# Attention, soft MoE and a gated product: the first pairs' loads, squares and stackings in another order

## The chip, the cores and the metric

The kernel runs on one core of a Trainium2 chip. The metric is the device time of one execution in microseconds, as the median of several runs. The engines are called by the profile's names: PE multiplies matrices, DVE, ACT and POOL work element by element, and SP issues the transfers.

## The reference, cut to what matters

```python
def _attn_ref(q, k, v, g_q, g_k):            # q, k, v: 4 x 12 x 448 x 64, float32
    def rmsnorm(x, g):
        rms = np.sqrt(np.mean(x * x, axis=-1, keepdims=True) + 1e-06)
        return x / rms * g
    q_n, k_n = (rmsnorm(q, g_q), rmsnorm(k, g_k))
    scores = scale * np.matmul(q_n, k_n.transpose(0, 1, 3, 2))
    scores = scores - np.max(scores, axis=-1, keepdims=True)
    attn = np.exp(scores)
    attn = attn / (np.sum(attn, axis=-1, keepdims=True) + 1e-09)
    return np.matmul(attn, v)
```

The result, as 1792 tokens of 768 values, goes through a soft mixture of 8 experts of 4 slots each (two softmaxes over the same logits, two products for each expert) and then through `(x @ w_a) * (x @ w_b) @ w_out` with an inner size of 1536. The change touches the attention alone.

## The kernel before, in words

**Tiling.** The 48 heads are 24 pairs. For a pair, q and k are loaded as one slot of `qk_sb` (112 partitions, 512 values of q and 512 of k; three slots take turns), v as one tile. Then, for q and for k: the squares (`square`), their sums by head and token (`sumsq`, tile `ssq`), the inverse root (`rsqrt`, tiles `nt` and `rinv`; ACT makes Ln and Exp, DVE refines it in three small steps, lines L288, L290 and L292), the product with it (`normalise`, tile `n`, L301), four transposes on PE and a split into a high and a low part (`emit_T`, tile `e`, lines L325 to L331), and six transfers from `e` into the two stacked tiles `z` of the pair's heads (`emit_Z`, lines L343 to L345), which is called the stacking here. `e` has one buffer, or two with the second pair's.

**The loop.** A head has four blocks of 112 queries, so a pair has eight steps. A step n issues `score(n + 2)` (two products, L358 and L359, and the maximum on DVE, L360), `expo(n + 1)` (the exponential on ACT, L369) and `ptrans(n)` (four transposes, L382, and an eviction by ACT or, in steps 1 and 5, by DVE). Around these the program puts the products with v of the pair before, and the preparation of pairs 2 to 4 ahead. In steps 5 and 7 the sums for pair j + 4 are taken; their squares are made by POOL (L255).

**Before the loop** the preparation of pairs 0 to 3 is written out: loads of pairs 0 to 2, squares by ACT (`prep`), roots (`norm`), `normalise`, `emit_T` and `emit_Z` of pairs 0 and 1, the load of pair 4 ahead of the second pair's stacking in SP's queue, then 15 products whose result nobody reads (`warm`, `W1`), the roots of pairs 2 and 3 and the first two scores.

**Order.** On PE, ACT, POOL and SP the attention's instructions stand in the order in which the program is written. DVE's order is made by a scheduler when the kernel is built. Every engine works through its own row strictly from the front.

Of the kernel before, what the change touches and what calls it, by code (L numbers as in the profile page):

```python
# [10 lines left out]
F32 = mybir.dt.float32  # L11
# [4 lines left out]
ALU = mybir.AluOpType  # L16
# [16 lines left out]
def kernel(  # L33
    ctx: ExitStack,
    tc: tile.TileContext,
    q: bass.AP,
    k: bass.AP,
    v: bass.AP,
    g_q: bass.AP,
    g_k: bass.AP,  # L40
# [5 lines left out]
):  # L46
    nc = tc.nc
    pe, act, dve, pool, sp = nc.tensor, nc.scalar, nc.vector, nc.gpsimd, nc.sync
    B, H, S, D = q.shape
    NT, DM = out.shape  # L50
    E, F = w1.shape[0], 1024
    NS = phi.shape[1]
    DF = 128 * len(LAGS)
    NC = 4
    P = S // NC
    HP = H // 2
    NPAIR = B * HP
    KD = DM // 128
# [21 lines left out]
    W3 = 2  # L80
    W4 = 7
    W5 = 3
    W1 = 15
    DV = 7
    P2_ENGINES = {ET.PE, ET.SP}

# [6 lines left out]
    ident = const.tile([128, 128], F32, name="ident")  # L93
# [10 lines left out]
    gg, g4, l_run, tb, ssq_eps = few[:, 0:1], few[:, 1:3], few[:, 3:4], few[:, 4:6], few[:, 6:7]  # L104
# [78 lines left out]
    def warm(ps, n):  # L183

        for _ in range(n):
            pe.matmul(ps[:, 0:128], ident, ident, start=True, stop=True)

    cring = ctx.enter_context(ExitStack())
    qk_sb = xw[1]
    extra = cring.enter_context(tc.tile_pool(name="extra", bufs=1)).tile([128, 3072], F32, name="extra")  # L190
    with ExitStack() as c1:
# [28 lines left out]
        def load_qk(p):  # L220
            if p >= NPAIR:
                return
            b, hp = divmod(p, HP)
            t = qk_sb[0:P, p % 3 * 1024:(p % 3 + 1) * 1024].rearrange("p (i h x) -> p i h x", i=2, h=2)
            for i, src in enumerate((q, k)):
                sp.dma_start(out=t[:, i], in_=src[b, 2 * hp:2 * hp + 2].rearrange("h (p c) d -> p h (c d)", c=NC))
            qk_t[p] = t

        def load_v(p):
            if p >= NPAIR:  # L230
                return
            b, hp = divmod(p, HP)
            src = v[b, 2 * hp:2 * hp + 2].rearrange("h (p c) d -> p h c d", c=NC)
            if p < NPAIR - 1:
                t = vp.tile([P, 2, NC, D], F32, tag="v", name=f"v{p}")
                sp.dma_start(out=t, in_=src)
                v_t[p] = [t[:, hd] for hd in range(2)]
            else:
                x = tk.tile([128, S], F32, tag="l4", name="v23a", bufs=1)[0:P, 0:NC * D]
                y = tk.tile([P, 4, 2, 32], F32, tag="c2", name="v23b", bufs=1)  # L240
                v_t[p] = x.rearrange("p (c d) -> p c d", d=D), y.rearrange("p c (a e) s -> p c (a e s)", a=2)
                for hd in range(2):
                    sp.dma_start(out=v_t[p][hd], in_=src[:, hd])

        sq_t = {}

        def square(p, i, eng=None):
            if p >= NPAIR:
                return
            sq = sqp.tile([P, 512], F32, tag="sq", name="sq")  # L250
            a = qk_t[p][:, i].rearrange("p h x -> p (h x)")
            if eng is act:
                act.activation(out=sq, in_=a, func=AF.Square)
            else:
                pool.tensor_tensor(out=sq, in0=a, in1=a, op=ALU.mult)  # L255
            sq_t[p, i] = sq
# [38 lines left out]
        def normalise(p, eng=None):  # L295
            if p >= NPAIR:
                return
            assert not any(x[0] == p for x in small)
            n_t[p] = npp.tile([P, 2, NC, 2, D], F32, tag="n", name=f"n{p}")
            for i in range(2):  # L300
                (eng if eng and i == 0 else pool).tensor_tensor(  # L301
                    out=n_t[p][:, i].rearrange("p c h d -> p h c d"),
                    in0=qk_t[p][:, i].rearrange("p h (c d) -> p h c d", d=D),
                    in1=rinv_t[p][:, i, :].rearrange("p (h c) -> p h c", h=2).unsqueeze(3).to_broadcast(
                        [P, 2, NC, D]
                    ),
                    op=ALU.mult,
                )
            qk_t.pop(p)

        def emit_T(p, i):
            if p >= NPAIR:
                return
            if i == 0:
                if p == 1:
                    e_t[p] = ring_p.tile([128, NU], F32, tag="wu", name="e1").bitcast(F32R)[:, 0:4 * S].rearrange(
                        "p (x s) -> p x s", s=S
                    )
                else:
                    e_t[p] = ep.tile([128, 4, S], F32R, tag="e", name=f"e{p}")  # L320
            et = e_t[p]
            src = n_t[p]
            ps = ps_m.tile([128, 512], F32, tag="m", name="pst")[:, 0:S]
            for c in range(NC):
                pe.transpose(ps[:, c * P:(c + 1) * P], src[:, i, c].rearrange("p h d -> p (h d)"), ident[0:P, 0:P])  # L325
            if i == 0:
                act.activation(out=et[:, 0], in_=ps, func=AF.Copy)
                dve.tensor_tensor(out=et[:, 3], in0=ps, in1=et[:, 0].bitcast(F32), op=ALU.subtract)
            else:
                act.activation(out=et[:, 1], in_=ps, func=AF.Copy, scale=gg)  # L330
                dve.scalar_tensor_tensor(  # L331
                    out=et[:, 2], in0=ps, scalar=gg, in1=et[:, 1].bitcast(F32), op0=ALU.mult, op1=ALU.subtract
                )
                n_t.pop(p)

        def emit_Z(p):
            if p >= NPAIR:
                return
            et = e_t.pop(p)
            for hd in range(2):  # L340
                z = zt[(2 * p + hd) % NZ]
                src = et[hd * D:(hd + 1) * D].bitcast(F32)
                sp.dma_start(out=z[0:D, 0:3].bitcast(F32), in_=src[:, 0:3])  # L343
                sp.dma_start(out=z[D:128, 0].bitcast(F32), in_=src[:, 3])
                sp.dma_start(out=z[D:128, 1:3].bitcast(F32), in_=src[:, 1:3])  # L345
# [201 lines left out]
        def norm(p):  # L547
            rsqrt(p)
            tick(3)

        def prep(p):
            for i in range(2):
                square(p, i, act)
                sumsq(p, i)
# [4 lines left out]
        for i, g in enumerate((g_q, g_k)):  # L559
            for r in range(2):  # L560
                sp.dma_start(out=g4[r * D:(r + 1) * D, i:i + 1], in_=g.rearrange("(d o) -> d o", o=1))
        dve.scalar_tensor_tensor(
            out=gg, in0=g4[:, 0:1], scalar=float(D) ** 0.5, in1=g4[:, 1:2], op0=ALU.mult, op1=ALU.mult
        )
        load_qk(2)
        load_v(0)
        sp.dma_start(out=phi_sb, in_=phi.rearrange("(k p) s -> p k s", p=128))
        prep(0)
        norm(0)
        prep(1)  # L570
        normalise(0, dve)
        load_qk(3)
        emit_T(0, 0)
        emit_T(0, 1)
        emit_Z(0)
        norm(1)
        normalise(1, dve)
        load_qk(4)
        prep(2)
        emit_T(1, 0)  # L580
        emit_T(1, 1)
        emit_Z(1)
        warm(ps_s.tile([128, 512], F32, tag="s", name="warm"), W1)
        norm(2)
        normalise(2)
# [595 lines left out]
            split(i + 2)  # L1181


_INS = ["q", "k", "v", "g_q", "g_k", "moe_phi", "moe_w1", "moe_w2", "moe2_w"]
_OUTS = [((1792, 768), "float32")]


# [35 lines left out]
```

## Time and profile before

| what | value |
|---|---|
| median of 3 runs | 591.48 us (590.6 to 592.62) |
| the profiled execution: its own time | 593.33 us |
| its span, first to last instruction | 591.5 us |
| PE busy | 557.4 us, 94% |
| ACT busy, DVE busy, POOL busy | 359.6, 349.6, 114.0 us |

The time of an execution is 1.9 us more than the span of its instructions. A share of busy time is a mean over stages: in the first 25 us PE waits for others, in the rest of the attention it hardly waits, and from about 330 us on the weights' transfers and then PE again set the pace.

### The profile page before, as it was taken

The page shows a single profiled execution, that of the slowest core. Times are in us where ns is not written, and L with a number is a line of the kernel's source. Part 1 is how long each engine was busy: PE and PEld are TensorE (multiplying, and loading weights), DVE is VectorE, ACT ScalarE, POOL GpSimd, SP SyncE. Part 2 cuts the span into 40 slices and gives each one's busy share as a digit, 9 for nine tenths or more (in the row PEclk, how much of TensorE's full clock was granted, in tenths as well). Part 3 has the DMA queues.
Part 4 walks back from the last instruction along what each step waited for, and adds up shares of the span by engine and source line. Part 5 has one row for each costly group of instructions (what it writes and reads, how often), then busy time and mean ns, then how long its engine had stood idle before and what let it go on. Part 6 is the DMA issues. An engine that isn't in the chain of part 4 may idle for free.

```text
span 591.5 us, 10977 instructions
## 1 busy us (share of the span) xinstructions
PE 557.4 (94%) x3980; PEld 366.9 (62%) x3980; DVE 349.6 (59%) x703; ACT 359.6 (61%) x845; POOL 114.0 (19%) x136
## 2 busy tenths in 40 slices
PE   5989999999999999999999998898989999999997
PEld 5755555566565665655656554343665656689996
DVE  5877777678787687776767521122228888842210
ACT  4677787787887787877877721111169899432210
POOL 1233433333433333333110000010100000200000
PEclk9899999999999999999999999989989999999999
DMA  7955677788697978697676689999999993002332
GB/s 176 220 142 140 165 175 168 209 235 223 165 261 153 266 178 240 166 271 188 156 216 170 271 330 351 426 395 425 428 423 421 418 406 144 1 28 80 92 94 83
DMA packets 39573, 134.51 MB, mean 227 GB/s; under 512 B 5856, under 2 KB 25312, under 8 KB 33120
## 3 DMA queue, kind: packets, MB, share of 16 engines
q1 hardware_dynamic: 39520, 133.81, 72.0%
q8 instruction: 32, 0.52, 0.4%
q14 instruction: 21, 0.17, 0.1%
HBM read 95.26 MB, written 5.51 MB: 170 GB/s over the span
## 4 chain that ended last, share of the span: by engine, by line
PE 75%; DMA 10%; DVE 4%; ACT 4%; SPq 3%; issue 2%; ACTq 0%; DVEq 0%
PE psv L396 12%; PE pspt L382 11%; PE pss L358 5%; DMA z<-e 5%; PE pss L359 5%; PE psM L938 5%; DMA wu_w<-in_moe_w_dram 5%; PE pso L1138 3%; PE pso L1140 3%; PE pso L1139 3%; PE psS L721 3%; PE psh L697 3%; PE pst L325 3%; PE psS L938 2%; PE psx L509 2%
## 5 line engine op out<-in xcount | busy, mean ns | idle before, releaser
L360 DVE TENSOR_REDUCE nmx<-pss 112x1 f32<-112x448 f32 x192 | 118.4, 619 | 40.9 <-PE pss L359 40.5
L369 ACT ACTIVATE p<-pss,nmx 112x448 f32<-112x448 f32 x192 | 123.7, 644 | 9.2 <-DVE nmx L360 6.3
L382 PEld LDWEIGHTS pspt<-ident,p 112*112 112x112 f32 x768 | 80.4, 133 | 78.9 <-ACT pt L388 27.5
L382 PE MATMUL pspt<-ident,p 112*112 112x112 f32 x768 | 110.0, 266 | 1.5 <-ACT p L369 1.4
L388 ACT COPY pt<-pspt 112x448 f32<-112x448 f32 x144 | 76.9, 534 | 27.1 <-PE pspt L382 25.6
L396 PE MATMUL psv<-pt,v 112*64 112x448 f32 x368 | 90.3, 569 | 0.0
L358 PE MATMUL pss<-z 128*112 128x448 f32 x192 | 85.1, 443 | 0.0
L301 POOL TENSOR_TENSOR n<-xw,rinv 112x512 f32<-112x512 f32 x46 | 47.1, 1043 | 174.7 <-PE pst L325 109.7
L359 PE MATMUL pss<-z 128*112 128x448 f32 x192 | 70.5, 367 | 0.0
L386 DVE COPY pt<-pspt 112x448 f32<-112x448 f32 x48 | 29.9, 623 | 20.9 <-PE pspt L382 20.8
L255 POOL TENSOR_TENSOR sq<-xw 112x512 f32<-112x512 f32 x40 | 40.9, 1041 | 5.4 <-DMA xw<-in_q_dram 4.9
L369 ACT ACTIVATION_READ_ACCUMULATOR p<-pss,nmx 112x1 f32 x192 | 40.0, 208 | 0.0
L1138 PE MATMUL pso<-Mh,t 128*128 128x384 f32 x112 | 37.9, 338 | 0.5 <-DVE Ml L967 0.5
L358 PEld LDWEIGHTS pss<-z 128*112 128x112 f32 x192 | 34.0, 177 | 6.7 <-issue 5.8
L1139 PE MATMUL pso<-Ml,t 128*128 128x384 f32 x112 | 37.7, 337 | 0.0
L1140 PE MATMUL pso<-Mh,t 128*128 128x384 f32 x112 | 37.7, 337 | 0.0
L325 PE MATMUL pst<-ident,n 112*128 112x112 f32 x192 | 27.1, 267 | 10.9 <-ACT rd L427 6.3
L1157 DVE COPY ot<-pso 128x384 f32<-128x384 f32 (+1 forms) x14 | 7.6, 543 | 49.5 <-PE pso L1142 49.5
L396 PEld LDWEIGHTS psv<-pt,v 112*64 112x64 f32 x368 | 18.3, 135 | 29.5 <-issue 22.4
L359 PEld LDWEIGHTS pss<-z 128*112 128x112 f32 x192 | 34.2, 178 | 0.7 <-issue 0.6
L938 PE MATMUL psM<-w,G 128*128 128x512 f32 x64 | 33.8, 610 | 0.8 <-DVE w L818 0.8
L818 DVE SCALAR_TENSOR_TENSOR xw<-wu_w,top 128x768 int32<-128x768 int32 x24 | 22.3, 953 | 19.6 <-ACT top L804 19.6
(177 smaller groups left out, 891.7 us busy)
## 6 DMA issues: line engine op xcount, KB each, us to landing
wu_w<-in_moe_w_dram SPq DMA_DIRECT2D x38, 1536.0 KB, 11.0
z<-e SPq DMA_DIRECT2D x48, 336.0 KB, 4.6
z<-e SPq DMA_DIRECT2D x48, 224.0 KB, 4.4
r<-in_moe_w_dram SPq DMA_DIRECT2D x7, 1536.0 KB, 8.6
xw<-in_moe_w_dram SPq DMA_DIRECT2D x4, 1536.0 KB, 13.7
xw<-in_q_dram SPq DMA_DIRECT2D x24, 224.0 KB, 4.5
xw<-in_k_dram SPq DMA_DIRECT2D x24, 224.0 KB, 4.0
z<-e SPq DMA_DIRECT2D x48, 112.0 KB, 4.4
```

Of the source, the lines that this page charges most:

```text
L301: (eng if eng and i == 0 else pool).tensor_tensor(out=n_t[p][:, i].rearrange("p c h d -> p h c d"), in0=qk_t[p][:, i].rearrange("p h (c d) ...
L358: pe.matmul(ps, x, z[:, 1, :], start=True, stop=False)
L359: pe.matmul(ps, x, z[:, 2, :], start=False, stop=True)
L360: dve.tensor_reduce(out=nm_of[n // 8][:, h % 2, c:c + 1], in_=ps, axis=AX.X, op=ALU.max, negate=True)
L369: act.activation(out=t, in_=ps_of.pop(n), func=AF.Exp, bias=nm_of[n // 8][:, h % 2, c:c + 1], accum_out=den_t[n // 8][:, h % 2, c:c + 1],)
L382: pe.transpose(ps[:, kc * P:(kc + 1) * P], src[:, kc * P:(kc + 1) * P], ident[0:P, 0:P])
L388: act.copy(out=o, in_=i)
L396: pe.matmul(av_t[p][hd * D:(hd + 1) * D, 0:S], v_t[p][hd][:, kc, :], pt_t[2 * p + hd][:, kc, :], start=(kc == 0), stop=(kc == NC - 1),)
L938: pe.matmul(o, G[:, r], W[:, c], start=st, stop=sp_)
L1138: pe.matmul(o, ch[:, m], Mh[:, m, c], start=(m == 0), stop=False)
L1139: pe.matmul(o, ch[:, m], Ml[:, m, c], start=False, stop=False)
L1140: pe.matmul(o, cl[:, m], Mh[:, m, c], start=False, stop=False)
```

## The change

Four things change. q and k of a pair are packed by the host into one array whose 4 KB for a partition lie together, and v into one with 2 KB, where a run was 1 KB before; a pair's q and k are one transfer, except the first pair's, which stay two. `square` and `normalise` read the packed order, the tile `n` keeps its own. The number of unread products ahead of the first score goes from 15 to 4. In the program's text `load_qk(4)` and `prep(2)` (squares and sums of pair 2) move behind the second pair's `emit_T` and `emit_Z`, while `load_qk(3)` stays where it was. And `normalise(0)` stands ahead of `prep(1)`, with the product of the two gains between them.

```diff
-    W1 = 15
+    W1 = 4
...
-            b, hp = divmod(p, HP)
-            t = qk_sb[0:P, p % 3 * 1024:(p % 3 + 1) * 1024].rearrange("p (i h x) -> p i h x", i=2, h=2)
-            for i, src in enumerate((q, k)):
-                sp.dma_start(out=t[:, i], in_=src[b, 2 * hp:2 * hp + 2].rearrange("h (p c) d -> p h (c d)", c=NC))
-            qk_t[p] = t
+            qk_t[p] = qk_sb[0:P, p % 3 * 1024:(p % 3 + 1) * 1024].rearrange("p (i x) -> p i x", i=2)
+            if p == 0:
+                for i in range(2):
+                    sp.dma_start(out=qk_t[p][:, i], in_=qk[p][:, i])
+            else:
+                sp.dma_start(out=qk_t[p], in_=qk[p])
...
-                sp.dma_start(out=t, in_=src)
+                sp.dma_start(out=t, in_=v[p])
...
-        dve.scalar_tensor_tensor(
-            out=gg, in0=g4[:, 0:1], scalar=float(D) ** 0.5, in1=g4[:, 1:2], op0=ALU.mult, op1=ALU.mult
-        )
         load_qk(2)
         load_v(0)
         sp.dma_start(out=phi_sb, in_=phi.rearrange("(k p) s -> p k s", p=128))
         prep(0)
         norm(0)
+        normalise(0, dve)
+        dve.scalar_tensor_tensor(
+            out=gg, in0=g4[:, 0:1], scalar=float(D) ** 0.5, in1=g4[:, 1:2], op0=ALU.mult, op1=ALU.mult
+        )
         prep(1)
-        normalise(0, dve)
         load_qk(3)
         emit_T(0, 0)
         emit_T(0, 1)
         emit_Z(0)
         norm(1)
         normalise(1, dve)
-        load_qk(4)
-        prep(2)
         emit_T(1, 0)
         emit_T(1, 1)
         emit_Z(1)
+        load_qk(4)
+        prep(2)
         warm(ps_s.tile([128, 512], F32, tag="s", name="warm"), W1)
```

What this makes of the queues shows in three places.

**DVE, first pairs.** The rows from the first pair's sums (`ssq_184`, in the changed kernel `ssq_181`) to the first split of `e`; `few` is the product of the gains, `ssq_198` and `ssq_199` are pair 1's sums. Before:

```order
L263 TENSOR_REDUCE ssq_184<-sq 112x8 x2
L288 SCALAR_TENSOR_TENSOR nt<-rinv_189 112x16
L290 SCALAR_TENSOR_TENSOR nt<-ssq_184,nt 112x16
L292 SCALAR_TENSOR_TENSOR rinv_189<-nt,rinv_189 112x16
L263 TENSOR_REDUCE ssq_198<-sq 112x8
L562 SCALAR_TENSOR_TENSOR few<-few 128x1
L301 TENSOR_TENSOR n_203<-xw_65,rinv_189 112x2x4x64
L263 TENSOR_REDUCE ssq_198<-sq 112x8
L328 TENSOR_TENSOR e_208<-pst,e_208 128x448
```

The same place in the changed kernel:

```order
L264 TENSOR_REDUCE ssq_181<-sq 112x8 x2
L289 SCALAR_TENSOR_TENSOR nt<-rinv_186 112x16
L565 SCALAR_TENSOR_TENSOR few<-few 128x1
L291 SCALAR_TENSOR_TENSOR nt<-ssq_181,nt 112x16
L264 TENSOR_REDUCE ssq_199<-sq 112x8
L293 SCALAR_TENSOR_TENSOR rinv_186<-nt,rinv_186 112x16
L264 TENSOR_REDUCE ssq_199<-sq 112x8
L302 TENSOR_TENSOR n_193<-xw_65,rinv_186 112x512
L325 TENSOR_TENSOR e_205<-pst,e_205 128x448
```

The first sum of pair 1 now stands ahead of the first pair's finished root, and the second ahead of its `n`.

**DVE, first scores.** The rows around the maxima `nmx` of the first head's scores; `ssq_297` (now `ssq_282`) are pair 3's sums, `ssq_412` (now `ssq_396`) pair 4's. Before:

```order
L263 TENSOR_REDUCE ssq_297<-sq 112x8
L288 SCALAR_TENSOR_TENSOR nt<-rinv_302 112x16
L290 SCALAR_TENSOR_TENSOR nt<-ssq_297,nt 112x16
L292 SCALAR_TENSOR_TENSOR rinv_302<-nt,rinv_302 112x16
L360 TENSOR_REDUCE nmx<-pss 112x1 x3
L263 TENSOR_REDUCE ssq_412<-sq 112x8 x2
L360 TENSOR_REDUCE nmx<-pss 112x1
L386 COPY pt_329<-pspt 112x4x112
L360 TENSOR_REDUCE nmx<-pss 112x1 x4
```

The changed kernel:

```order
L357 TENSOR_REDUCE nmx<-pss 112x1
L291 SCALAR_TENSOR_TENSOR nt<-ssq_260,nt 112x16
L264 TENSOR_REDUCE ssq_282<-sq 112x8 x2
L293 SCALAR_TENSOR_TENSOR rinv_270<-nt,rinv_270 112x16
L289 SCALAR_TENSOR_TENSOR nt<-rinv_287 112x16
L291 SCALAR_TENSOR_TENSOR nt<-ssq_282,nt 112x16
L293 SCALAR_TENSOR_TENSOR rinv_287<-nt,rinv_287 112x16
L357 TENSOR_REDUCE nmx<-pss 112x1
L383 COPY pt_313<-pspt 112x4x112
L264 TENSOR_REDUCE ssq_396<-sq 112x8
L357 TENSOR_REDUCE nmx<-pss 112x1
L264 TENSOR_REDUCE ssq_396<-sq 112x8
```

Three maxima moved ahead of pair 3's sums (the last of the three is the first row here), and pair 4's two sums now stand ahead of the fifth and of the sixth maximum, which follows the last row.

**SP, the stackings.** The rows from the last transfer of the first pair's stacking (into `z_142`) on; `z_143` and `z_144` are the second pair's, and the `xw` rows are loads of q and k, of pair 4 and then of pair 5. Before:

```order
L345 DMA z_142<-e_208 64x896
L226 DMA xw_65<-in_q_dram 112x2x256
L226 DMA xw_65<-in_k_dram 112x2x256
L343 DMA z_143<-e_248 64x1344
L344 DMA z_143<-e_248 64x448
L345 DMA z_143<-e_248 64x896
L343 DMA z_144<-e_248 64x1344
L344 DMA z_144<-e_248 64x448
L345 DMA z_144<-e_248 64x896
L226 DMA xw_65<-in_q_dram 112x2x256
```

The changed kernel:

```order
L342 DMA z_142<-e_205 64x896
L340 DMA z_143<-e_236 64x1344
L341 DMA z_143<-e_236 64x448
L342 DMA z_143<-e_236 64x896
L340 DMA z_144<-e_236 64x1344
L341 DMA z_144<-e_236 64x448
L342 DMA z_144<-e_236 64x896
L230 DMA xw_65<-in_qk_dram 112x1024 x2
```

Pair 4's load moved from ahead of the second pair's stacking to behind it; the two loads of the last row are pair 4's and pair 5's.

## Rows read from the trace of the kernel before

**Rows 1.** The page, part 1: busy time, share and instructions of each engine.

```profile
PE 557.4 (94%) x3980; PEld 366.9 (62%) x3980; DVE 349.6 (59%) x703; ACT 359.6 (61%) x845; POOL 114.0 (19%) x136
```

**Rows 2.** Stretches of the span, with granted clock, DMA share and rate.

```profile
core 0: us, PE busy (x) PEld busy (x) DVE busy (x) ACT busy (x) POOL busy (x), PEclk, DMA share, GB/s
2.20:5.00 2.80, 2.80 (x16) 2.80 (x15) 0.68 (x1) 1.47 (x5) 0.00 (x0) 1.00 1.01 288
...
43.70:47.00 3.30, 3.30 (x12) 1.33 (x11) 2.16 (x5) 1.88 (x6) 1.72 (x2) 0.50 0.33 70
60.00:100.00 40.00, 37.12 (x237) 22.06 (x236) 28.40 (x62) 31.15 (x87) 15.41 (x18) 1.00 0.69 163
100.00:200.00 100.00, 98.75 (x654) 59.60 (x653) 75.34 (x165) 79.53 (x217) 33.34 (x36) 1.00 0.83 216
200.00:330.00 130.00, 126.96 (x845) 77.85 (x846) 96.00 (x206) 100.82 (x275) 34.60 (x38) 1.00 0.77 208
395.00:398.00 3.00, 2.92 (x29) 1.35 (x32) 1.25 (x3) 0.80 (x2) 1.13 (x1) 0.54 0.98 418
```

**Rows 3.** The chain that ended last, 20 to 50 us: start, length, what.

```profile
22.04 1.59 DVE nmx L360 x3
23.64 1.19 DVE ssq L263 x2
...
36.94 4.42 DMA z<-e
...
45.02 1.69 PE psv L396 x4
...
48.64 0.90 PE psv L396 x4
```

**Rows 4.** Timeline of ACT: the first, fifth and sixth exponential.

```profile
22.61 0.64 ACT L369 ACTIVATE p<-pss,nmx 112x448 f32<-112x448 f32 x1 [2.85 <-DVE nmx L360]
...
26.51 0.65 ACT L369 ACTIVATE p<-pss,nmx 112x448 f32<-112x448 f32 x1
...
27.55 0.66 ACT L369 ACTIVATE p<-pss,nmx 112x448 f32<-112x448 f32 x1
```

**Rows 5.** Timeline of POOL: pair 4's squares of q and of k.

```profile
20.76 1.04 POOL L255 TENSOR_TENSOR sq<-xw 112x512 f32<-112x512 f32 x1
21.96 1.04 POOL L255 TENSOR_TENSOR sq<-xw 112x512 f32<-112x512 f32 x1 [0.16 <-DVE nt L290]
```

**Rows 6.** Timeline of SP: the first issue of each stacking, and the load behind it.

```profile
11.38 0.50 SPq L343 DMA_DIRECT2D z<-e  x1
...
17.09 0.53 SPq L226 DMA_DIRECT2D xw<-in_q_dram  x1
...
18.47 0.47 SPq L343 DMA_DIRECT2D z<-e  x1
...
24.40 0.53 SPq L226 DMA_DIRECT2D xw<-in_q_dram  x1
```

**Rows 7.** Timeline of DVE, 7 to 15 us.

```profile
7.05 0.69 DVE L263 TENSOR_REDUCE ssq<-sq 112x8 f32<-112x512 f32 x1
...
8.18 0.68 DVE L301 TENSOR_TENSOR n<-xw,rinv 112x512 f32<-112x512 f32 x1
...
12.91 1.30 DVE L301 TENSOR_TENSOR n<-xw,rinv 112x512 f32<-112x512 f32 x1
```

**Rows 8.** Transfers, issue to landing in us: the first load, and that of 24.40.

```profile
xw<-in_q_dram SPq DMA_DIRECT2D x1, 224.0 KB, 2.9
...
xw<-in_q_dram SPq DMA_DIRECT2D x1, 224.0 KB, 4.9
```

**Rows 9.** Timeline of PE: the unread products and the first score.

```profile
15.87 5.39 PE L186 MATMUL warm<-ident 128*128 128x128 f32 x30
21.02 0.44 PE L358 MATMUL pss<-z 128*112 128x448 f32 x1
```

**Rows 10.** Waits of ACT, 40 to 335 us: sum, times, longest.

```profile
ACT e L327 <- DMA z<-e: 8.9, 6, 2.8
```

More of the change, by code (lines that the diff above doesn't have):

```diff
@@ L35 @@
     tc: tile.TileContext,
-    q: bass.AP,
-    k: bass.AP,
+    qk: bass.AP,
     v: bass.AP,
@@ L48 @@
     pe, act, dve, pool, sp = nc.tensor, nc.scalar, nc.vector, nc.gpsimd, nc.sync
-    B, H, S, D = q.shape
     NT, DM = out.shape
+    D = g_q.shape[0]
+    NC = 4
+    P = qk.shape[1]
+    S = NC * P
+    B = NT // S
+    H = DM // D
     E, F = w1.shape[0], 1024
@@ L53 @@
     DF = 128 * len(LAGS)
-    NC = 4
-    P = S // NC
     HP = H // 2
@@ L231, in load_v @@
                 return
-            b, hp = divmod(p, HP)
-            src = v[b, 2 * hp:2 * hp + 2].rearrange("h (p c) d -> p h c d", c=NC)
             if p < NPAIR - 1:
                 t = vp.tile([P, 2, NC, D], F32, tag="v", name=f"v{p}")
-                sp.dma_start(out=t, in_=src)
+                sp.dma_start(out=t, in_=v[p])
                 v_t[p] = [t[:, hd] for hd in range(2)]
@@ L242, in load_v @@
                 for hd in range(2):
-                    sp.dma_start(out=v_t[p][hd], in_=src[:, hd])
+                    sp.dma_start(out=v_t[p][hd], in_=v[p][:, hd])
         sq_t = {}
@@ L250, in square @@
             sq = sqp.tile([P, 512], F32, tag="sq", name="sq")
-            a = qk_t[p][:, i].rearrange("p h x -> p (h x)")
+            a = qk_t[p][:, i]
             if eng is act:
@@ L298, in normalise @@
             assert not any(x[0] == p for x in small)
-            n_t[p] = npp.tile([P, 2, NC, 2, D], F32, tag="n", name=f"n{p}")
+            n_t[p] = npp.tile([P, 2, 8, D], F32, tag="n", name=f"n{p}")
             for i in range(2):
                 (eng if eng and i == 0 else pool).tensor_tensor(
[L302 to L307, printed above, removed]
+                    out=n_t[p][:, i], in0=qk_t[p][:, i].rearrange("p (n d) -> p n d", d=D),
+                    in1=rinv_t[p][:, i].unsqueeze(2).to_broadcast([P, 8, D]), op=ALU.mult,
                 )
@@ L324, in emit_T @@
             for c in range(NC):
-                pe.transpose(ps[:, c * P:(c + 1) * P], src[:, i, c].rearrange("p h d -> p (h d)"), ident[0:P, 0:P])
+                pe.transpose(ps[:, c * P:(c + 1) * P], src[:, i, 2 * c:2 * c + 2].rearrange("p h d -> p (h d)"), ident[0:P, 0:P])
             if i == 0:
@@ L1181 @@
             split(i + 2)
-_INS = ["q", "k", "v", "g_q", "g_k", "moe_phi", "moe_w1", "moe_w2", "moe2_w"]
+_INS = ["qk", "v", "g_q", "g_k", "moe_phi", "moe_w1", "moe_w2", "moe2_w"]
 _OUTS = [((1792, 768), "float32")]
@@ L1207 @@
     arrays, args = {}, []
+    q, k, v = (inputs.pop(x) for x in "qkv")
+    b, h, n, d = q.shape
+    q, k, v = (x.reshape(b, h // 2, 2, n // 4, 4, d) for x in (q, k, v))
+    qk = _np.stack([x.transpose(0, 1, 3, 4, 2, 5) for x in (q, k)], axis=3)
+    inputs["qk"] = qk.reshape(b * h // 2, n // 4, 2, 8 * d)
+    inputs["v"] = v.transpose(0, 1, 3, 2, 4, 5).reshape(b * h // 2, n // 4, 2, 4, d)
     inputs["moe2_w"] = _in_units(*(inputs.pop(f"moe2_w_{x}") for x in ("a", "b", "out")))
```

## The prediction

> **What bounds the kernel now.** I read the page first: PE is busy 94% of the span [rows 1], so a gain has to come from where PE waits. The table of stretches shows where: from 60 to 330 us PE idles 2.88 + 1.25 + 3.04 = 7.2 us in all [rows 2], and the change removes no work of PE's but eleven unread products. Then I read the chain that ended last through the first 50 us, since the change lies there. It doesn't go through the unread products or the first scores' products. It runs over DVE: three maxima one behind the other, pair 4's two sums, the next maximum, and then over ACT's exponentials [rows 3]. The reader is to see that the first score started at 21.02 [rows 9], that its exponential began at 22.61, and that exponentials 5 and 6 followed at 26.51 and 27.55, about one in 1.04 us [rows 4]. Later the chain passes through a stacking's last transfer, 36.94 plus 4.42 us, for which ACT's split of the next pair waits [rows 3]. That transfer follows from the pair's transposes, which stand behind the sixth exponential in PE's row, so whatever delays that exponential delays all that follows. From there on the loop's steps hang on one another, and the weights' loads are issued at fixed steps of it. I therefore count a shift of the sixth exponential in full at the end.
>
> **Fewer unread products.** 30 recorded halves took 5.39 us; 15 products become 4, that is 30 halves become 8, which frees 22/30 x 5.39 = 3.95 us of PE ahead of the first score [rows 9]. The score's result is used by DVE and ACT, though. In ACT's row the roots of pair 3 still stand ahead of the first exponential, and they wait for pair 3's sums on DVE, which now stand behind three maxima. So of the 3.95 us I let nothing through on its own; what the first exponential gains is lost again further on, as follows.
>
> **Pair 4's load behind the second stacking.** This is the term that decides. SP issues a stacking in 17.09 - 11.38 = 5.71 us and the next in 24.40 - 18.47 = 5.93 us, one issue behind the other [rows 6]. Before, pair 4's load went out at 17.09 between the two, and POOL could square it at 20.76 and 21.96 [rows 5]. Now it goes out after both: the start of the first stacking plus 5.71 + 5.93 = 11.64 us.
>
> That start: it was 11.38 [rows 6]. In the changed DVE row one of pair 1's sums, 0.69 us, stands ahead of the first root [rows 7], and the q half of `n`, 0.68 us alone, took 1.30 us where POOL's half ran beside it [rows 7]; so POOL's half starts 0.7 later and DVE's follows it. Against that, the first loads come in longer runs. The rate with 1 KB runs was 288 GB/s, that of the weights' 12 KB runs 418 [rows 2]; one load of 224 KB takes 0.80 us at the one and 0.55 at the other, so 0.2 us comes back. I take a start 0.5 later, 11.9, with bounds of 0 and +0.7. The product of the gains only changes its place in this stretch, and its wait for its own loads is covered by ACT's root, which DVE awaits there anyway; uncovered it would cost the upper bound. The second stacking could start as soon as pair 1's split is done, but SP is still issuing the first then, so the earlier squares or splits of pair 1 buy nothing at SP.
>
> Pair 4's load is then issued at 11.9 + 11.64 = 23.5. The shortest time to landing was 2.9 us, for the first load with nothing ahead of it; the load at 24.40, in the same place behind a stacking, took 4.9 us, with one load more ahead of it than there will be [rows 8]. I take 3.7, so it lands at 27.2. The bounds are 11.4 + 11.64 + 2.9 = 25.9 and 12.1 + 11.64 + 4.9 = 28.6.
>
> Behind the landing stand, one after the other: POOL's square of q, 1.04 us [rows 5]; DVE's sum, 1.19/2 = 0.60 us, and the fifth maximum, 1.59/3 = 0.53 us [rows 3]; then the second sum and the sixth maximum, 0.60 + 0.53 (POOL's square of k ends at 2.08 and is ready by then). With 0.1 us for the handovers that is 3.4 us. The sixth exponential can start at 27.2 + 3.4 = 30.6 where it started at 27.55: **+3.1 us**, bounds 25.9 + 3.4 - 27.55 = +1.75 and +4.45. What is queued behind these two sums on DVE are all later maxima, and ACT and PE have nothing else to do: three score buffers are full by then.
>
> **Clock.** PE will idle between the third score and the first exponential, and again before the fifth. Before, the wait for the stacking that landed at 36.94 + 4.42 = 41.4 was followed by a stretch at half the clock, 1.2 GHz, 0.50 from 43.7 to 47.0, in which four products with v took 1.69 us where they took 0.90 at 48.64 [rows 2, 3]. If that comes after 30 us, a step's PE work of about 0.9 us becomes about 1.5 and outgrows the 1.04 us of a step: two to three steps at 0.5 each, so 0 to 1.5 us. The next stacking's wait swallows what falls behind the transposes of pair 2. I take **+0.5**.
>
> **Packed loads in the loop.** A pair loads 672 KB: 2.39 us at 288 GB/s, 1.65 at 418 [rows 2], so 0.74 us less transfer for each pair. It counts only where something waits on transfers: ACT waited 8.9 us in 6 places for a stacking [rows 10]. Upper bound 6 x 0.74 = 4.4 us, lower bound nothing, since a pair's v, q and k are issued behind the stacking that is awaited and can only get in its way at its tail. Nearer to nothing: **-0.6**. One issue less for each pair on SP (0.53 us [rows 6]) is hidden, as SP waits for DVE's split ahead of each stacking; uncovered it would be that much for each pair.
>
> The Trainium skill sees less in the longer runs: "DMA: Bandwidth & Descriptors", section "Why small descriptors are slow (HBM only)", gives about 3 cycles for a packet beside one for each 32 bytes. By it a run of 1 KB costs 35 and one of 4 KB 131, an estimate of 6% instead of the 31% between the two rates; the term would be -0.1 and the time 595.0. No row here shows a load of q or k in longer runs.
>
> **Sum.** +3.1 + 0.5 - 0.6 = +3.0 us. The profiled execution would go from 593.33 to 596.3; it was 1.85 us above the median of the runs shown, so the median goes from 591.48 to **594.5 us**. All bounds together: 591.48 + 1.75 - 4.4 = 588.8 and 591.48 + 4.45 + 1.5 = 597.4.
>
> **Rivals.**
> *The first score decides, faster.* If the exponentials follow the scores and pair 4's sums don't hold the maxima, the 3.95 us come through: 591.48 - 3.95 - 0.6 = 586.9. For it: PE stood in unread products until 21.02 [rows 9]. Against it: DVE's row, and SP's issue times. It holds from the point where pair 4's load lands by 27.55 - 3.4 = 24.15 and pair 3's roots are done 4 us earlier; for that SP would have to issue the load at 21.25, 2.3 us before I expect it. Chance 0.15.
> *The packed loads pay in full, no measurable change.* All six waits shrink by 0.74 us: 591.48 + 3.6 - 4.4 = 590.7. For it: the transfers' share of 0.69 to 0.83 in the loop [rows 2]. Against it: the loads stand behind the stacking. Chance 0.18.
> *The clock costs more, slower.* If PE stays at the lower clock through the first pair, beyond the 1.5 us: another 2 us, 596.5. For it: both idle times follow each other closely. Against it: by 48.64 the products were back at 0.90 us [rows 3]. The Trainium skill ("TensorE: Matmul & The Clock Gate", "What's actually happening") calls the lower clock the default, which only activity lifts; by that rule the eleven products removed make this likelier. Chance 0.10.
> *The start comes out even:* landing near its lower bound and some gain in the loop, 592. Chance 0.05.
>
> **How the numbers follow.** My forecast has 0.52. A difference under 0.3% (1.8 us) is what a measurement of this kernel can't tell from none. Slower: forecast and clock, 0.62. Same: the even start and most of the packed loads' case, 0.20. Faster: the first rival and a rest of the packed loads' case, 0.18. The range goes from 588.8, the sum's lower bound, which takes in the packed loads' case, to 598.4, the clock's case with its own spread; what lies outside is the first rival and a little above.
>
> **What would show it.** In the profile after: the load of pair 4 issued by SP at 23 to 24 and POOL's first square of pair 4 not before 26; DVE idle ahead of a sum of pair 4 for some 2 us, with POOL's square named as what it waited for; ACT's fifth and sixth exponential 2 to 4 us later than before, though the first score starts near 17; every later pair shifted by as much. It is wrong if POOL squares pair 4 by 24, or if the waits for stackings between 40 and 330 us fall by several us.

## The result, and the profile after

| | kernel before | changed kernel |
|---|---|---|
| median | 591.11 us (590.6 to 592.62) | 598.43 us (598.18 to 598.91) |
| ratio, 95% interval | | 1.0126 [1.0107, 1.0145] |
| the profiled execution: its own time, span | 593.33, 591.5 us | 598.91, 596.8 us |

The change costs 7.3 us where 3.0 were forecast: the direction is right, the size is not, and the median lies a hair above the range's upper end (598.4). The profiled spans differ by 5.3 us only, because the execution profiled before was 2.2 us above its median. Up to the first exponential of the last pair they differ by more: it stands at 325.11 before and at 332.94 now, 7.8 us later.

The page's first line reads like that of before [rows 1]: less unread work on PE, the same everywhere else. It doesn't show where the time went.

```profile
PE 558.0 (93%) x3958; PEld 367.6 (62%) x3958; DVE 350.0 (59%) x703; ACT 360.0 (60%) x845; POOL 114.3 (19%) x136
```

The timeline of SP shows the first issue of both stackings and, behind the second, the loads of pairs 4 and 5 (start, length, what):

```profile
13.86 0.50 SPq L340 DMA_DIRECT2D z<-e  x1
...
19.57 0.54 SPq L340 DMA_DIRECT2D z<-e  x1
...
25.44 1.42 SPq L230 DMA_DIRECT2D xw<-in_qk_dram  x2
```

The first stacking starts at 13.86, not at 11.38 [rows 6] and not at the 11.9 of the forecast. From there to the load are 11.58 us; 11.64 had been worked out. The timeline of DVE shows what made the start late:

```profile
6.14 0.17 DVE L289 SCALAR_TENSOR_TENSOR nt<-rinv 112x16 f32<-112x16 f32 x1 [0.69 <-ACT rinv L288]
8.75 0.16 DVE L565 SCALAR_TENSOR_TENSOR few<-few 128x1 f32<-128x1 f32 x1 [2.44 <-DMA few<-in_g_k_dram]
8.82 0.17 DVE L291 SCALAR_TENSOR_TENSOR nt<-ssq,nt 112x16 f32<-112x16 f32 x1
```

ACT's root was there at 6.14, and the next step of the root stood ready; but the product of the gains, now ahead of it, waited 2.44 us for the loads of g. The chain that ended last then shows what follows pair 4's load (start, length, what):

```profile
25.44 5.72 DMA xw<-in_qk_dram
...
31.30 1.05 POOL sq L256
...
32.37 0.69 DVE ssq L264
33.06 0.54 DVE nmx L357
...
33.68 0.73 ACT p L366 x2
...
45.46 4.46 DMA z<-e
```

This is the chain of the forecast, link for link, but with 5.72 us in the place of 3.7 for the landing. ACT's first, fourth, fifth, sixth and ninth exponential:

```profile
24.24 0.62 ACT L366 ACTIVATE p<-pss,nmx 112x448 f32<-112x448 f32 x1
...
27.57 0.63 ACT L366 ACTIVATE p<-pss,nmx 112x448 f32<-112x448 f32 x1 [0.39 <-PE pspt L379]
33.68 0.63 ACT L366 ACTIVATE p<-pss,nmx 112x448 f32<-112x448 f32 x1 [4.13 <-DVE nmx L357]
...
34.80 0.63 ACT L366 ACTIVATE p<-pss,nmx 112x448 f32<-112x448 f32 x1
...
39.63 0.64 ACT L366 ACTIVATE p<-pss,nmx 112x448 f32<-112x448 f32 x1
```

The sixth is 7.25 us later than at 27.55 [rows 4], the ninth 8.27 later than at 31.36. The stretches, to be held beside [rows 2]:

```profile
2.20:5.00 2.80, 2.80 (x16) 2.80 (x15) 0.90 (x2) 1.59 (x5) 0.00 (x0) 1.00 0.87 282
...
28.00:31.30 3.30, 3.22 (x13) 2.31 (x11) 0.15 (x1) 0.83 (x3) 0.00 (x1) 0.51 0.81 237
30.00:40.00 10.00, 6.76 (x37) 5.38 (x35) 5.83 (x10) 5.28 (x14) 2.88 (x3) 0.77 0.08 21
60.00:100.00 40.00, 39.37 (x256) 23.82 (x252) 30.56 (x67) 31.75 (x87) 13.96 (x15) 1.00 0.70 173
100.00:200.00 100.00, 97.18 (x640) 58.93 (x638) 76.13 (x164) 79.36 (x216) 36.05 (x39) 1.00 0.76 199
200.00:330.00 130.00, 127.06 (x850) 78.22 (x848) 96.14 (x207) 101.59 (x279) 35.19 (x39) 1.00 0.77 205
```

From 60 to 330 us PE idles 0.63 + 2.82 + 2.94 = 6.4 us; it was 7.2. In the first loads the packed runs (2 KB for pair 0, 4 KB for pair 1) moved 282 GB/s, the runs of 1 KB 288; but the DMA engines were busy 0.87 of that stretch now and 1.01 before, so it doesn't compare the two forms. And PE ran at 1.2 GHz (0.51) ahead of the stall.

### The profile page after: what moved, and what is told of

It reads as the page before. It is cut to its first block, busy times and chain, and to the rows that moved or that the text cites. A ratio compares the mean times of both kernels' runs of the same rounds, so it can differ in the third digit from the quotient of the medians.

```text
span 596.8 us, 10870 instructions
## 1 busy us (share of the span) xinstructions
PE 558.0 (93%) x3958; PEld 367.6 (62%) x3958; DVE 350.0 (59%) x703; ACT 360.0 (60%) x845; POOL 114.3 (19%) x136
## 4 chain that ended last, share of the span: by engine, by line
PE 77%; DMA 10%; ACT 4%; DVE 4%; SPq 3%; issue 1%; POOL 0%; ACTq 0%; DVEq 0%; POOLq 0%
PE psv L393 13%; PE pspt L379 12%; PE pss L355 6%; PE pss L356 5%; DMA wu_w<-in_moe_w_dram 5%; PE psM L935 4%; DMA z<-e 4%; PE pso L1135 3%; PE pso L1136 3%; PE pso L1137 3%; PE psS L718 3%; PE pst L322 3%; PE psh L694 3%; PE psS L935 2%; PE psx L506 2%; PE psab L863 2%
## 5 line engine op out<-in xcount | busy, mean ns | idle before, releaser
L379 PEld LDWEIGHTS pspt<-ident,p 112*112 112x112 f32 x768 | 82.3, 136 | 85.4 <-ACT pt L385 28.2
L366 ACT ACTIVATE p<-pss,nmx 112x448 f32<-112x448 f32 x192 | 123.5, 643 | 11.9 <-DVE nmx L357 8.5
L379 PE MATMUL pspt<-ident,p 112*112 112x112 f32 x768 | 112.2, 269 | 7.7 <-ACT p L366 7.7
L355 PE MATMUL pss<-z 128*112 128x448 f32 x192 | 87.2, 454 | 0.5 <-DMA z<-e 0.5
L356 PE MATMUL pss<-z 128*112 128x448 f32 x192 | 72.3, 376 | 0.0
L355 PEld LDWEIGHTS pss<-z 128*112 128x112 f32 x192 | 35.1, 183 | 7.6 <-issue 7.3
L264 DVE TENSOR_REDUCE ssq<-sq 112x8 f32<-112x512 f32 x48 | 32.3, 676 | 6.3 <-POOL sq L256 4.2
L356 PEld LDWEIGHTS pss<-z 128*112 128x112 f32 x192 | 35.3, 184 | 0.7 <-issue 0.6
```

The source lines that it names most:

```text
L355: pe.matmul(ps, x, z[:, 1, :], start=True, stop=False)
L356: pe.matmul(ps, x, z[:, 2, :], start=False, stop=True)
L366: act.activation(out=t, in_=ps_of.pop(n), func=AF.Exp, bias=nm_of[n // 8][:, h % 2, c:c + 1], accum_out=den_t[n // 8][:, h % 2, c:c + 1],)
L379: pe.transpose(ps[:, kc * P:(kc + 1) * P], src[:, kc * P:(kc + 1) * P], ident[0:P, 0:P])
```

## The experiments

Each run was timed against the kernel before on the same chip; the ratio is to that. In these series the kernel before measured 591.7 to 592.1 us, in the first, with the changed kernel, 591.1; a difference of medians to the changed kernel is therefore up to 1 us too small, and the ratios are the better guide. The last columns are from its profiled execution; before, the first stacking was issued at 11.38 [rows 6], pair 4 squared at 20.76 [rows 5], and the sixth exponential began at 27.55 [rows 4].

| run | median, us | ratio, 95% interval | first stacking | POOL squares pair 4 | sixth exponential |
|---|---|---|---|---|---|
| changed kernel | 598.43 | 1.0126 [1.0107, 1.0145] | 13.86 | 31.30 | 34.80 |
| e1_gains_act | 595.84 | 1.0066 [1.0034, 1.0098] | 11.47 | 28.68 | 32.72 |
| e2_load4_early | 592.49 | 1.0010 [0.9991, 1.0028] | 13.07 | 25.34 | 29.97 |
| e3_two_loads | 593.75 | 1.0028 [0.9999, 1.0057] | 11.23 | 26.84 | 30.34 |
| e4_packed_only | 593.25 | 1.0022 [0.9996, 1.0049] | 14.27 | 25.32 | 30.80 |
| e5_before_w4 | 589.38 | 0.9953 [0.9925, 0.9982] | 11.58 | 21.19 | 25.58 |
| e6_after_w15 | 594.35 | 1.0048 [1.0026, 1.0070] | 12.23 | 29.89 | 26.18 |
| e7_order_only | 593.70 | 1.0048 [1.0023, 1.0072] | 11.50 | 27.09 | 30.59 |
| e8_gains_load4 | 591.08 | 0.9989 [0.9962, 1.0015] | 11.96 | 23.45 | 28.16 |
| e9_all_three | 591.35 | 0.9997 [0.9965, 1.0030] | 12.10 | 24.28 | 28.77 |
| e12_squares_back | 589.07 | 0.9946 [0.9922, 0.9969] | 12.60 | 22.21 | 27.29 |
| e13_before_w4_again | 589.58 | 0.9950 [0.9929, 0.9972] | 11.36 | 20.73 | 25.33 |
| e14_moved_unread | 590.00 | 0.9968 [0.9950, 0.9986] | 11.38 | 22.14 | 27.71 |

**The two causes, one at a time.** First the gains' product alone, taken out of DVE's row:

```diff
-        dve.scalar_tensor_tensor(
-            out=gg, in0=g4[:, 0:1], scalar=float(D) ** 0.5, in1=g4[:, 1:2], op0=ALU.mult, op1=ALU.mult
-        )
...
         emit_T(0, 0)
+        act.activation(out=gg, in_=g4[:, 0:1], func=AF.Copy, scale=g4[:, 1:2])
+        act.activation(out=gg, in_=gg, func=AF.Copy, scale=float(D) ** 0.5)
```

> The changed kernel with the product of the two gains made by two ACT copies ahead of the first k half's split, so that DVE's row no longer holds it ahead of the first root. Theory (pair 4's landing holds the sixth exponential, and the wait for the gains delays everything ahead of it): the first stacking starts at 11.6 instead of 13.86, the sixth exponential 2.2 us sooner than 34.80, time 598.4 - 2.2 = 596.2. Rival (the 4 KB runs as such are slow, in the loop too): no change, 598.4. Rival (PE at the lower clock for want of unread products): no change, 598.4.

595.84: 2.6 us less than the changed kernel by the medians, 3.5 by the ratios. The first stacking is back at 11.47, and POOL's row still names the load:

```profile
28.68 2.04 POOL L256 TENSOR_TENSOR sq<-xw 112x512 f32<-112x512 f32 x2 [5.02 <-DMA xw<-in_qk_dram]
```

Then pair 4's load alone, put back ahead of the second stacking:

```diff
         normalise(1, dve)
+        load_qk(4)
         emit_T(1, 0)
         emit_T(1, 1)
         emit_Z(1)
-        load_qk(4)
         prep(2)
```

> The changed kernel with pair 4's load back ahead of the second stacking in SP's queue; DVE's row is the same, word for word. Theory: the load goes out near 19.5 instead of 25.4, POOL squares pair 4 right behind pair 2's product near 26, the sixth exponential starts near 29.9 instead of 34.80, time 598.4 - 4.9 = 593.5. Rival (4 KB runs): the same bytes in the same runs, 598.4. Rival (clock): 598.4 or a little less.

592.49: 5.9 us less by the medians, 6.9 by the ratios, and POOL waits for no load any more; pair 2's `n`, which stands ahead of pair 4's squares in its row, now sets their time:

```profile
23.34 2.04 POOL L302 TENSOR_TENSOR n<-xw,rinv 112x512 f32<-112x512 f32 x2 [8.11 <-DVE rinv L293]
25.34 2.04 POOL L256 TENSOR_TENSOR sq<-xw 112x512 f32<-112x512 f32 x2
```

The granted clock was 0.50 from 24 to 28 us in this run too, and yet the time is that of before within 0.3%: a low clock while PE has slack costs little. DVE, which had no gap from 23.71 us to the sixth maximum, set the pace here. Its fifth maximum ended at 28.6 and the fifth exponential began at 28.79, some 0.2 us later, because ACT's copy ahead of it had waited for transposes at the low clock:

```profile
28.00 0.61 DVE L357 TENSOR_REDUCE nmx<-pss 112x1 f32<-112x448 f32 x1
```

```profile
28.36 0.53 ACT L385 COPY pt<-pspt 112x448 f32<-112x448 f32 x1 [0.57 <-PE pspt L379]
```

Both repairs together:

> The changed kernel with both repairs: the product of the gains made by two ACT copies, so that DVE does not wait for it, and pair 4's load ahead of the second stacking again. Theory (the two causes add up and are all): first stacking at 11.5, pair 4's load at 17.2, its first square on POOL near 23.8, now behind pair 2's normalisation and not behind the load, sixth exponential near 28.4, time 591.2 (590.4 to 592.0), no measurable difference to the kernel before. Rival (4 KB runs or fewer unread products cost something by themselves): 593 and more in spite of a sixth exponential by 28.5.

591.08, as expected, and no difference to before that can be measured. The two repairs give back the whole loss against the kernel before. They don't undo every cost of the new order: the kernel before gains some 2 us by 4 unread products alone (below), and this one, which has them too, does not show that gain; the last version below says where a part of it went.

**Packed loads against order.** Two runs share out the change: the packed arrays in the order of before, with 15 unread products; and the new order with 4 products and the loads of before.

> The kernel before with the packed loads alone: 15 unread products, the old order of the program. The scheduler puts the gains' product ahead of the first root here too. Theory: the first stacking starts some 2 us later, pair 4's load still goes out between the stackings and holds nothing, time 591.1 + 2 = 593. Rival (4 KB runs are the cause): all of the loss is here, 598.4. Rival (clock): 591.

> The changed kernel's order and its 4 unread products with the old loads, two for each pair in runs of 1 KB. The scheduler keeps the gains' product behind the first root here. Theory: first stacking near 11.9, pair 4's q and k issued from 23.5 and landed near 27.6, sixth exponential near 31.1, time 591.1 + 3.6 = 594.7. Rival (4 KB runs): no loss, 591. Rival (clock): all of the loss, 598.

593.25 and 593.70. In the first the gains' product fell ahead of the root as well and waited 2.06 us there; in the second it fell one step behind the root and did not wait. The load is squared 4.06 us after its issue in the second (23.03 to 27.09), 5.86 after it in the changed kernel. So the packed form alone brings nothing (1.5 us lost by the medians, with an interval that reaches no change), and the new order alone loses 2 us. I had not separated these two before: the late gains and the late landing belong to the packed form, the late issue to the order. The two losses add up to 3.5 of the 7.3 us only; the rest appears only where both meet, with the load behind both stackings, where a late start and a late landing both delay the square.

**The length of the runs.** The changed kernel, but q and k of every pair as two transfers of 2 KB for a partition:

```diff
-            if p == 0:
-                for i in range(2):
-                    sp.dma_start(out=qk_t[p][:, i], in_=qk[p][:, i])
-            else:
-                sp.dma_start(out=qk_t[p], in_=qk[p])
+            for i in range(2):
+                sp.dma_start(out=qk_t[p][:, i], in_=qk[p][:, i])
```

> The changed kernel with every pair's q and k loaded as two transfers of 2 KB a partition in place of one of 4 KB. The product of the gains then falls one root step further back in DVE's row. Theory (the long runs land late; they hold the gains and pair 4): the gains are awaited for under 1 us, first stacking issued at 11.5 to 12, pair 4's q load at 23 to 23.6 and landed some 4 us later, POOL's first square of pair 4 at 27 to 27.6, sixth exponential near 30.6, time 593.7 (593.0 to 594.6), as with the old loads in the changed order. Rival (the place in the queue makes both late, not the length of the runs): gains awaited for 2 us and more, landing 5.7, square of pair 4 at 29 to 31, time 596 to 598.4.

593.75, 4.7 us less than the changed kernel (5.8 by the ratios), by nothing but the cut of the transfers and the place of the gains' product that the scheduler drew from it. The timelines of DVE and POOL:

```profile
6.79 0.17 DVE L290 SCALAR_TENSOR_TENSOR rinv<-nt,rinv 112x16 f32<-112x16 f32 x1
6.90 0.69 DVE L261 TENSOR_REDUCE ssq<-sq 112x8 f32<-112x512 f32 x1
7.50 0.61 DVE L562 SCALAR_TENSOR_TENSOR few<-few 128x1 f32<-128x1 f32 x1
...
26.84 2.04 POOL L253 TENSOR_TENSOR sq<-xw 112x512 f32<-112x512 f32 x2 [4.16 <-DMA xw<-in_qk_dram]
```

The square starts 4.25 us after the issue (22.59). The transfers from issue to landing, first of the changed kernel (gains, then the loads of pairs 4 and 5), then of this run:

```profile
few<-in_g_k_dram SPq DMA_DIRECT2D x2, 0.2 KB, 4.3
...
xw<-in_qk_dram SPq DMA_DIRECT2D x2, 448.0 KB, 5.9
```

```profile
few<-in_g_k_dram SPq DMA_DIRECT2D x2, 0.2 KB, 2.5
...
xw<-in_qk_dram SPq DMA_DIRECT2D x3, 224.0 KB, 4.1
```

From issue to square the changed kernel takes 1.6 us longer. Some 0.6 of it is that the one transfer brings k too, for which the first square needn't wait: the second half, issued 0.7 later, lands 4.7 after the first issue. The other 1.0 us comes with the single transfer, but this run doesn't say by what: beside the longer runs, pair 5's load goes out 0.64 us behind pair 4's in the changed kernel and 1.7 us behind it here, and moves at the same time. Both pairs together were there 6.7 us after the first issue in the changed kernel and 6.3 after it here. The rate as such did not differ. Stretches in which only loads of q and k moved, of the changed kernel (4 KB) and of e7_order_only (1 KB):

```profile
28.00:30.00 2.00, 2.00 (x10) 1.74 (x9) 0.15 (x1) 0.83 (x3) 0.00 (x0) 0.50 0.96 299
```

```profile
26.00:28.00 2.00, 1.54 (x8) 0.92 (x7) 0.00 (x0) 0.48 (x1) 0.92 (x1) 0.82 1.07 303
```

The gains stand behind the loads of pairs 0 and 1; the last of them was there at 8.6 us in the changed kernel and at 6.9 in this run.

With two transfers on top of both repairs:

> As the run with both repairs, and every pair's q and k as two transfers of 2 KB a partition. Theory: pair 4's landing no longer holds anything here, so the time is that of the run with both repairs within 0.6 us (590.6 to 591.8). Rival (long runs cost time in the loop as well, pair by pair): 1 to 3 us less than the run with both repairs, with less waiting of ACT for stackings between 40 and 330 us.

591.35, the same as e8 within the intervals: where nothing waits for pair 4's landing, the length of the runs costs and gives nothing that these runs can measure, in the loop neither.

**The unread products.** The kernel before with `W1 = 4`, and nothing else:

> The kernel before with 4 unread products in place of 15 and nothing else; the maxima of the first scores move ahead of pair 3's second root step in DVE's row, pair 4's sums behind them. Theory (what costs time is pair 4's landing and the first stacking, both as before here): first score at 17 to 17.5, POOL's first square of pair 4 near 20.8 as before, sixth exponential at 24.5 to 26.5, time 588.5 to 590.5. Rival one (idle PE ahead of the exponentials costs clock): the granted clock from 22 to 40 us is near 0.5 and the time 591.5 to 593. Rival two (the first exponential waits for pair 3's roots, so the score's earlier start is lost): sixth exponential within 0.7 us of 27.55 and the time 590.8 to 591.8.

589.38, faster than before, and again in a second run:

> The kernel before with 4 unread products, a second time, beside the run above. If its gain is real: 588.5 to 590.3 and a ratio of 0.995 to 0.998; if it was chance: within 0.2% of the kernel before.

589.58. Timelines of POOL and ACT in the first of them; the load stays early, so the sixth exponential comes 1.97 us sooner:

```profile
21.19 2.15 POOL L255 TENSOR_TENSOR sq<-xw 112x512 f32<-112x512 f32 x2 [0.20 <-DMA xw<-in_q_dram]
```

```profile
25.58 0.65 ACT L369 ACTIVATE p<-pss,nmx 112x448 f32<-112x448 f32 x1
```

The other way round, the changed kernel with `W1 = 15`:

> The changed kernel with 15 unread products again. DVE's order changes with it: six maxima now stand ahead of pair 4's first sum where four did, so that the landing holds the seventh and eighth exponential in place of the fifth and sixth. Theory (pair 4's landing decides, not the unread products and not the clock): load at 25.4 and POOL's square at 31.3 as in the changed kernel, eighth exponential near 34.8 where it was the sixth, so two steps of 1.04 us less, time 596.3 (595.3 to 597.5); more unread work, and yet faster. Rival one (idle PE costs clock): granted clock from 24 to 31 us near 1.0 and the time 594 or less. Rival two (the products themselves decide): 598.4 or more, since the first score comes 3 to 4 us later.

594.35, 4.1 us less than with 4 products, 2 us below what I expected and near the clock rival's bound. DVE's and ACT's rows show one part of the miss: the gains were awaited for 0.78 us in this execution, so stacking, load and square came 1.4 to 1.7 us earlier than in the changed kernel.

```profile
7.12 0.16 DVE L565 SCALAR_TENSOR_TENSOR few<-few 128x1 f32<-128x1 f32 x1 [0.78 <-DMA few<-in_g_k_dram]
```

```profile
26.18 0.66 ACT L366 ACTIVATE p<-pss,nmx 112x448 f32<-112x448 f32 x1
32.27 0.63 ACT L366 ACTIVATE p<-pss,nmx 112x448 f32<-112x448 f32 x1 [4.92 <-DVE nmx L357]
```

The landing does hold the seventh exponential here in place of the fifth. But PE also ran at full clock up to the stall (1.00 from 24 to 28 us, where the changed kernel had 0.55), so the rest of the miss may be the clock's. This run doesn't divide the two.

**A version with everything repaired.** Two transfers, gains on ACT, pair 4's load and pair 2's squares both ahead of the second split:

> The run with all three repairs, and the squares of pair 2 ahead of the second pair's split again, so that POOL reaches pair 4 earlier: of the change, the packed arrays, the four unread products and the earlier n of the first pair are left. Theory (the place of these squares is what still separates the repaired change from the kernel before with 4 unread products): POOL's first square of pair 4 near 21 to 22, sixth exponential at 25.3 to 26.3, time 589.4 (588.5 to 590.3). Rival (the packed arrays cost something): 591 or more in spite of an early square.

589.07. The square came at 22.21 and the sixth exponential at 27.29, 1 us later than expected in this execution, but the time is that of e5: the two are the best versions found, both faster than the kernel before, and the packed arrays add nothing to the smaller edit that could be measured. This run differs from e9 by the place of pair 2's squares alone. So that place was a third cost of the new order, 2.3 us by the medians (0.9997 against 0.9946, with intervals that just touch), which the earlier runs had not shown.

**A wait that depends on the unread products.** In all runs with 4 of them the shift of the exponentials against before falls by some 1.2 us between the first exponentials of pair 3 and of pair 4. ACT's first split for pair 5 waits there for pair 4's stacking: 1.94 us before, 0.69 to 0.76 us in the ten profiled executions with 4 products. Of before, then of e5:

```profile
67.92 0.54 ACT L327 ACTIVATE e<-pst 128x448 fp32r<-128x448 f32 x1 [1.94 <-DMA z<-e]
```

```profile
64.76 0.54 ACT L327 ACTIVATE e<-pst 128x448 fp32r<-128x448 f32 x1 [0.75 <-DMA z<-e]
```

The last run moves the other 11 products instead of leaving them out:

```diff
         emit_Z(0)
+        wt = ps_s.tile([128, 512], F32, tag="s", name="warm")
+        warm(wt, 11)
         norm(1)
...
-        warm(ps_s.tile([128, 512], F32, tag="s", name="warm"), W1)
+        warm(wt, W1)
```

> The kernel before with 4 unread products ahead of the first score, and the 11 others not left out but made earlier, between the first pair's transposes and the second's, where PE waits 4.5 us anyway. DVE's scheduler mixes the first three maxima a little more with pair 3's sums. What is asked: in three profiled kernels with 15 unread products ACT's split waits 1.8 to 2.1 us for the stacking of pair 2's successor near 66 to 70 us, in eight with 4 products 0.7 us. Theory (it is the number of instructions in PE's stream up to there, since a 16 KB transfer of instructions then lies beside that stacking): the wait is 1.7 to 2.1 us again and the time 590.6 (589.8 to 591.4), 1.2 us above the run with 4 products. Rival (it is the time at which the first scores run, which the 11 products shift): the wait is 0.7 us and the time 589.4 (588.6 to 590.2).

590.00, which lies in both ranges; the wait (for pair 4's stacking, not that of pair 2's successor) decides, and it is back:

```profile
68.13 0.54 ACT L327 ACTIVATE e<-pst 128x448 fp32r<-128x448 f32 x1 [2.00 <-DMA z<-e]
```

The awaited transfer took 5.67 us, from 62.35 on, and the view of transfers from 64 to 66 us shows beside it, as it does before at 62.20 plus 5.61:

```profile
q8 instruction: 1, 0.02, 3.0%
```

In e5 that transfer of instructions falls between 66 and 68 us, behind the stacking. So the wait follows the number of instructions in PE's stream, not the time of the first score. That the transfer of instructions is what delays the stacking fits all these rows, and the other traces too: of the last transfers of a stacking issued between 30 and 70 us in the fourteen profiled executions, the 12 with such a transfer (16 KB) well inside their course took 5.4 to 5.7 us, the 29 others 3.9 to 4.5. No run changed it alone.

## Why the prediction was wrong

| step | forecast | measured |
|---|---|---|
| first stacking starts | 11.9 (11.4 to 12.1) | 13.86 |
| from there to pair 4's load | 11.64 | 11.58 |
| the load lands after | 3.7 (2.9 to 4.9) | 5.72 |
| from landing to sixth exponential | 3.4 | 3.64 |
| sixth exponential | +3.1 (+1.75 to +4.45) | +7.25 |
| from there to the ninth (clock) | +0.5 (0 to 1.5) | +1.0 |
| packed loads in the loop | -0.6 (0 to -4.4) | 0 |
| pair 4's stacking (near 68 us) | not in the sum | -1.2 |
| sum | +3.0 | +7.1; medians +7.3 |

**The mechanism was right.** The load's new place in SP's queue decides, the maxima wait behind pair 4's sums, and the shift of the sixth exponential comes through nearly in full. Of the unread products I had let nothing of their 3.95 us through. In the changed kernel nothing did: the late stacking held the first score until 19.35, not near 17, and the first exponential came 1.6 us later than before. But their effect depends on the order. In the old one they are worth 2 us (e5), in the new one the kernel with 15 is the faster (e6): DVE's order then lets two more maxima pass ahead of pair 4's first sum. That the scheduler's order moves with their number was not in the prediction.

**The step that failed first** is the sentence on the gains: "its wait for its own loads is covered by ACT's root". It was not. The start came 2.0 us after the forecast and 2.4 after that of e1, which has no such wait; I had put "the upper bound" on it, 0.7. I had no row for either. The views of before could have given it, the issues of g_k, their landing and DVE's first step of the root:

```profile
3.93 1.24 SPq L561 DMA_DIRECT2D few<-in_g_k_dram  x2
```

```profile
few<-in_g_k_dram SPq DMA_DIRECT2D x2, 0.2 KB, 2.5
```

```profile
6.53 0.18 DVE L288 SCALAR_TENSOR_TENSOR nt<-rinv 112x16 f32<-112x16 f32 x1 [0.69 <-ACT rinv L287]
```

The last of them, issued at about 4.55, took 2.4 us, so the gains were there at about 6.9, and DVE's first step with ACT's root ended at 6.7. Some 0.2 us of wait was to be read off even without a later landing; with a last landing at 8.6 it became 2.4. e1 and e3 show the price from two sides.

**The second is a term's size**: the landing, taken as 3.7 with 4.9 as its upper bound. Both rows were of transfers half as large and of 1 KB runs [rows 8]; for such halves 3.7 was nearly right (3.9 in e7, 4.1 in e3). The changed load is one transfer of twice the size, and I had argued its longer runs as a gain only (224 KB in 0.55 instead of 0.80 us, by the weights' rate). I had also put the 4.9 of the load at 24.40 down to "one load more ahead of it"; but pair 4 had been squared at 20.76 and 21.96 [rows 5], so its loads had landed by then. The rate of 418 GB/s came from runs of 12 KB late in the kernel and didn't carry over: loads in 4 KB runs moved 299 GB/s, in 1 KB runs 303. The rule of the Trainium skill on packet sizes ("DMA: Bandwidth & Descriptors", "Why small descriptors are slow (HBM only)") gives an estimate of 6% less time for the longer runs, nearer than my 31%. These two rates don't show that gain, though the engines' share beside them, 0.96 against 1.07, is lower with the longer runs.

**The clock** cost 1.0, inside its bounds. The low clock of before the stall lasted beyond it: PE's four transposes took 0.95 us at 35.88 and 0.55 at 39.27, and ACT's split ahead of the eighth exponential waited for those of pair 2.

```profile
37.61 0.55 ACT L324 ACTIVATE e<-pst 128x448 fp32r<-128x448 f32 x1 [1.03 <-PE pst L322]
```

e2 had the same low clock ahead of 28 us and lost some 0.2 us by it; there it was back before the sixth exponential, and the shift didn't grow from that to the ninth (2.43 and 2.41). What costs is the low clock that outlasts a stall. **The packed loads' case** fell: ACT's waits for stackings between 40 and 330 us are 9.4 us in 8 places, where they were 8.9 in 6 [rows 10]. And for the -1.2 us of pair 4's stacking I had no row: it depends on how many instructions stand ahead of it. It hides a part of the miss; without it the loss would have been about 8.5 us.

## What to carry to other kernels

An instruction whose operands come by a transfer is not hidden because its engine waits there for something else: add the transfer's issue and landing and compare the sum with the moment at which the other wait ends. A load that is given a larger transfer must be priced by its landing, not by its bytes at the best rate seen elsewhere, and if one half of it is needed first, two transfers bring it sooner. And where one change bundles several edits, their effects needn't add up: fewer unread products gain 2 us in the old order and lose time in the new one, and packing and order lose 3.5 us apart and 7.3 together. The parts are worth running apart.

## What the runs showed of the hardware

Loads to 112 partitions in runs of 4 KB moved no faster than in runs of 1 KB: 299 against 303 GB/s where only such loads moved. Behind both stackings, one transfer of 448 KB landed 5.6 to 6.0 us after its issue in the three profiled executions that have it there (of the changed kernel, e1 and e6), while the first of two halves landed after 3.9 and 4.1 us and both after 4.7 (e7, e3). The small transfers of g, issued behind the loads of pairs 0 and 1, took 4.1 to 4.6 us to land (those of the second gain) in five of the six kernels in which pair 1 comes in 4 KB runs, 2.9 us in the sixth (e6), and 2.4 to 3.4 us in the eight executions with runs of 1 or 2 KB. A part of this is that they are issued 0.5 us sooner behind one transfer than behind two: the last of them was there at 7.0 to 8.6 us in the six, at 6.9 to 7.7 in the eight. The wait for them ahead of the first root was 0.78, 1.68, 2.06 and 2.44 us in four profiled executions. And eleven unread products more or less, whether made early or late, changed a wait for a transfer some 50 us later by 1.2 us.
